# An MLP's late part in two tiles of 768 tokens instead of three of 512, and six attention blocks instead of eight with transposed exponentials

## Chip, cores and metric

The kernel runs on one core of a Trainium2 chip. The metric is the device time of one execution in microseconds (us), taken as the median of several runs. TensorE multiplies matrices, VectorE (DVE) and ScalarE (ACT) work elementwise and empty PSUM, GpSimd (POOL) helps with SBUF-only work, and all transfers are issued by SyncE (SP).

## What is computed

Sparse causal attention over q, k, v of shape (4, 8, 576, 64), then two MLPs over 2304 tokens of width 512 with a hidden width of 2048, the first with a squared relu, the second with a SiLU:

```python
scores = scale * np.matmul(q, k.transpose(0, 1, 3, 2))
mask_plain = (rel >= 0) & (rel < 32)                       # heads 0 to 3
mask_dil = (rel >= 0) & (rel < 128) & (rel % 4 == 0)       # heads 4 to 7
attn = softmax(where(mask, scores, -1e9)); x = attn @ v
...
h = x @ w_in;  r = np.maximum(h, 0.0);  x = (r * r) @ w_out
h = x @ w2_in; g = h * (1.0 / (1.0 + np.exp(-h))); out = g @ w2_out
```

The weights arrive as float64 words, and the kernel turns them into float32 itself.

## The kernel before

**Numbers.** Every large product is made of three matmuls on high and low halves (hi x hi, hi x lo, lo x hi; `fp32r` tiles). A value is split by a copy (ScalarE, mostly) into its high half and a subtraction (VectorE or GpSimd) for the low half.

**Attention.** 32 blocks (`attention(h, pair)`): h is half a batch entry (288 queries), pair two heads. Pairs 0 and 1 have three units of 96 queries with 96 to 128 keys, pairs 2 and 3 four units of 72 queries with 72 or 104 keys. An ordinary block computes scores on TensorE (L533), masks them and takes the row maximum on VectorE (L558), exponentiates each unit on ScalarE with the maximum as bias and the sum accumulated (L566), normalises (L586, L590, L592), transposes on TensorE (L602), copies back to SBUF and multiplies with v (L625). The first `EARLY` blocks go by `late_exp` (L680): scores are transposed first, the exponential of all units together is one instruction per group on ScalarE reading PSUM (L729), v has a column of ones so that the value product (L738) brings the sums along, and the result is normalised (L751, L754) and turned (L630). The maximum is subtracted beforehand on VectorE or GpSimd (`less`, L691 to L695) in the first `AHEAD` blocks, and by two more matmuls per unit (L717) in the other early ones. `EARLY` is 8 and `AHEAD` is 4, so blocks 0 to 3 subtract beforehand, blocks 4 to 7 by matmul, the others are ordinary.

**First MLP.** `TILES[0]` has three tiles of 256 tokens, which `mlp` (L771) runs interleaved chunk by chunk with attention and the conversion of the weights (`weights`, L255), and then three tiles of 512 tokens run by `mlp2` (L908). `mlp2` does its first product in seven Strassen products of 42 matmuls with 256 columns per pair of chunks (L936, eight pairs), assembles them on VectorE (`a1` to `a4`, L952), squares (L972), splits, and does the second product plainly with 192 matmuls of 512 columns (L990 to L992). Its inputs are prepared by `load_x` (L856).

**Second MLP.** Three tiles of 768 tokens run by `strassen` (L1054): both products have seven Strassen products, with matmuls of 384 columns (L1094 for the first, L1182 for the second). Sums of weight blocks for the first products are made by `sums` (L362), those for the second by `sums2` (L403), both written to DRAM and streamed in again (`stream`, L438, `stream2`, L468). `load_xs` (L1009) prepares the input and its differences.

**Order.** The order of all instructions is written out in the table `ORDER` (L1361): each word is an engine letter, the number of an operation in the order of its creation, and the places of its buffers. A word F means that many matmuls on a constant tile (L1248) whose results nobody reads. Places of SBUF buffers are given by the pools of L40 to L46.

## Time and profile before

| | |
|---|---|
| runs | 849.41 us median of 3 (848.76 to 850.98) |
| profiled execution | 851.04 us, of which the span from the first to the last instruction is 849.3 |
| busy: TensorE, VectorE, ScalarE, GpSimd | 840.2 (99%), 681.8 (80%), 501.2 (59%), 121.9 us (14%) |
| DMA | 222.49 MB by the queue that SP issues, 75.6% of 16 engines' span |
| chain that ended last | PE 94%, ACT 4%, DVE 1% |
| waiting matmuls (F words) | 53, all ahead of the first MLP step |

In the page's second part each digit is the busy share of one fortieth of the span in tenths. Matmuls are pipelined, so a single one's length is more than what it adds; the distance from one start to the next is what counts. The groups of rows name the line of the program, the engine, the operation and the tiles written and read.

### The profile page before, as it was taken

The numbers are of one execution on the slowest core, as the hardware profiler recorded it, in microseconds if no ns is written. First come the engines' busy times: TensorE is split into PE (matmuls) and PEld (weight loads), VectorE is DVE, ScalarE is ACT, GpSimd is POOL, SyncE is SP. The second block draws the span as 40 slices with busy tenths as digits, with TensorE's granted clock in tenths as the row PEclk, the third lists the DMA queues.
The fourth block names the chain that finished last, engine by engine and source line by source line (L and its number), as shares of the span: only waits on it lengthen the run. The fifth ranks groups of instructions, "written<-read, shape, count | busy, mean of one in ns | idle before, by whom it ended". The sixth has DMA issues, their size and how long they took to land.

```text
span 849.3 us, 17021 instructions
## 1 busy us (share of the span) xinstructions
PE 840.2 (99%) x6009; PEld 796.2 (94%) x6009; DVE 681.8 (80%) x1754; ACT 501.2 (59%) x1324; POOL 121.9 (14%) x142
## 2 busy tenths in 40 slices
PE   8999999999999999999999999999999999999998
PEld 7879999999989889889998999999999999999998
DVE  5999999888888698768899998898735788437865
ACT  4999988888566255324543466575445555345652
POOL 2211000101210202131201002202200111201120
PEclk9999999999999999999999999999999999999999
DMA  9486558779888888998999999889774675871751
GB/s 343 164 281 221 152 188 319 257 275 333 317 293 305 315 286 286 335 318 278 332 348 313 324 315 357 298 282 319 248 266 149 240 262 168 269 265 41 243 159 65
DMA packets 83604, 223.56 MB, mean 263 GB/s; under 512 B 8768, under 2 KB 18240, under 8 KB 83520
## 3 DMA queue, kind: packets, MB, share of 16 engines
q1 hardware_dynamic: 83520, 222.49, 75.6%
q8 instruction: 47, 0.77, 0.3%
q14 instruction: 37, 0.30, 0.1%
HBM read 172.13 MB, written 50.33 MB: 262 GB/s over the span
## 4 chain that ended last, share of the span: by engine, by line
PE 94%; ACT 4%; DVE 1%; DMA 0%; issue 0%; POOL 0%; SPq 0%; POOLq 0%; ACTq 0%
PE y L1094 17%; PE sa L1182 15%; PE s L936 14%; PE y L1182 6%; PE y L990 5%; PE y L991 5%; PE y L992 5%; PE sa L1094 4%; PE s L788 3%; PE s L789 2%; PE s L790 2%; PE ax L533 2%; PE y L836 2%; PE ax L625 2%; PE y L837 2%; PE y L838 2%
## 5 line engine op out<-in xcount | busy, mean ns | idle before, releaser
L245 ACT CAST hl<-gq 128x384 fp32r<-128x384 f32 x168 | 79.5, 513 | 62.7 <-PE sa L1182 27.0
L1094 PE MATMUL y<-xs,ws 128*128 128x384 f32 x552 | 107.5, 334 | 0.0
L1094 PEld LDWEIGHTS y<-xs,ws 128*128 128x128 f32 x552 | 96.7, 188 | 0.1
L252 DVE TENSOR_TENSOR hl<-gq,hl 128x384 fp32r<-128x384 f32 x144 | 78.7, 581 | 17.6 <-ACT hl L245 14.5
L1070 ACT COPY gq<-y 128x384 f32<-128x384 f32 x92 | 42.6, 479 | 69.1 <-PE y L1094 61.7
L1182 PE MATMUL sa<-hl,wp 128*128 128x384 f32 x432 | 79.1, 334 | 0.0
L936 PE MATMUL s<-x,ws 128*128 128x256 f32 x576 | 76.2, 284 | 0.0
L990 PE MATMUL y<-g,w 128*128 128x512 f32 x192 | 76.2, 397 | 0.0
L952 DVE TENSOR_TENSOR h<-s,h 128x512 f32<-128x512 f32 x96 | 59.5, 621 | 20.8 <-PE s L936 17.4
L1182 PEld LDWEIGHTS sa<-hl,wp 128*128 128x128 f32 x432 | 75.3, 188 | 0.0
L991 PE MATMUL y<-g,w 128*128 128x512 f32 x192 | 75.2, 391 | 0.0
L992 PE MATMUL y<-g,w 128*128 128x512 f32 x192 | 74.9, 390 | 0.0
L245 ACT CAST g<-r 128x256 fp32r<-128x256 f32 (+1 forms) x86 | 42.9, 504 | 52.0 <-DVE r L972 46.0
L936 PEld LDWEIGHTS s<-x,ws 128*128 128x128 f32 x576 | 72.2, 191 | 1.2
L566 ACT ACTIVATE ap<-ap,ast 96x128 f32<-96x128 f32 (+3 forms) x168 | 62.2, 372 | 8.3 <-DVE ast L575 4.2
L1065 DVE TENSOR_TENSOR gq<-y,gq 128x384 f32<-128x384 f32 x46 | 25.0, 554 | 52.0 <-PE y L1094 45.7
L788 PE MATMUL s<-x,w 128*128 128x256 f32 x192 | 56.3, 293 | 0.1
L1133 DVE TENSOR_TENSOR gq<-gq,sg 128x768 f32<-128x768 f32 x48 | 46.9, 992 | 10.3 <-ACT sg L1131 10.3
L790 PE MATMUL s<-x,w 128*128 128x256 f32 x192 | 54.3, 283 | 0.0
L789 PE MATMUL s<-x,w 128*128 128x256 f32 x192 | 54.2, 282 | 0.0
L1182 PE MATMUL y<-hl,sw 128*128 128x384 f32 x288 | 51.4, 334 | 0.0
L1182 PE MATMUL sa<-hl,sw 128*128 128x384 f32 x288 | 50.9, 334 | 0.0
(177 smaller groups left out, 2123.6 us busy)
## 6 DMA issues: line engine op xcount, KB each, us to landing
raw<-w SPq DMA_DIRECT2D x64, 512.0 KB, 6.1
ws<-w1x SPq DMA_DIRECT2D x48, 512.0 KB, 6.4
ws<-w2x SPq DMA_DIRECT2D x48, 512.0 KB, 5.4
sw<-w2y SPq DMA_DIRECT2D x48, 512.0 KB, 4.6
wa<-w1s SPq DMA_DIRECT2D x24, 512.0 KB, 6.9
wa<-w2s SPq DMA_DIRECT2D x24, 512.0 KB, 5.8
w1x<-st SPq DMA_DIRECT2D x16, 512.0 KB, 5.2
w2x<-st SPq DMA_DIRECT2D x16, 512.0 KB, 4.4
```

Of the source, the lines that this page charges most:

```text
L245: self.nc.scalar.copy(out=out, in_=in_)
L252: self.eng[eng].tensor_tensor(out=out, in0=a, in1=b, op=ALU.subtract)
L566: es.append(self.op({"ACT": c_act(nk) + 0.185}, lambda e, i=i, n=n, c=c, p=p, st=st: nc.scalar.activation(out=p.tile[:n, c], in_=p.tile[:n ...
L788: nc.tensor.matmul(o, wh.tile[:, s], xh, start=(kk == 0), stop=False)
L789: nc.tensor.matmul(o, wh.tile[:, s], xl, start=False, stop=False)
L790: nc.tensor.matmul(o, wl.tile[:, s], xh, start=False, stop=(kk == KC - 1))
L936: nc.tensor.matmul(bank.tile[:, o:o + 256], wp, xp, start=i == 0, stop=last, skip_group_check=True)
L990: nc.tensor.matmul(o, wh.tile[:, s], gh.tile, start=c == 0, stop=False)
L991: nc.tensor.matmul(o, wh.tile[:, s], gl.tile, start=False, stop=False)
L992: nc.tensor.matmul(o, wl.tile[:, s], gh.tile, start=False, stop=(c == NF - 1))
L1094: nc.tensor.matmul(o, w[part == 2].tile[:, kk * P:kk * P + P], x[b][part == 1].tile[:, kk * half:kk * half + half], start=new and not kk a ...
L1182: nc.tensor.matmul(o, u.tile[:, c * P:c * P + P], v.tile, start=new and not q and not part, stop=q == nf - 1 and part == 2, skip_group_che ...
```

## The change

The late part of the first MLP goes by `strassen` in two tiles of 768 tokens. Tile 3, which is in `WHOLE`, does its second product plainly in the new function `whole`, in two halves of 384 tokens; tile 4 does both products by Strassen. For that the second weight matrix of the first MLP is kept in SBUF in 256-column halves (`second`), its blocks are put together again (`again`), their sums are made and written to DRAM (`sums2(0, f)`) and streamed in for tile 4. `mlp2` and `load_x` go. `EARLY` is 6 and `AHEAD` 2: blocks 2 and 3 subtract the maximum by matmul, blocks 6 and 7 are ordinary. The squared relu may run on ScalarE in two steps (`relu2`). Pools and shared areas of SBUF are cut anew, and the order table is another one (4279 words instead of 4017; its F words ask for 86 matmuls, 41 ahead of the first MLP step and 45 behind it).

```diff
-EARLY = 8
-AHEAD = 4
+EARLY = 6
+AHEAD = 2
...
-TILES = ([(0, 256), (256, 256), (512, 256), (768, 512), (1280, 512), (1792, 512)], [(0, 768), (768, 768), (1536, 768)])
+TILES = ([(0, 256), (256, 256), (512, 256), (768, 768), (1536, 768)], [(0, 768), (768, 768), (1536, 768)])
...
-POOLS = {"u2": (8, 512), "u3": (2, 512), "u4": (28, 1024), "w1": (16, 1024), "blk": (BLK_BUFS, 1280)}
-SHARED_LO = 91
-SHARED_HI = 205
+POOLS = {"u2": (8, 512), "u4": (29, 1024), "w1": (16, 512), "w1o": (8, 1024), "blk": (BLK_BUFS, 1280)}
+SHARED_LO = 16
+SHARED_HI = 203
...
+    def again(self, j, c, key, gate):
+        b = self.spot(("cw", "ct")[j], PIECE)
+        old = self.kept[0, c, j, "c"]
...
+        elif j:
+            o = None
+            for i, (wh, wl, d) in enumerate(self.wt[0, 1, c]):
+                o = self.op({"Pool": c_pool2(256), "DVE": c_dve(256)}, lambda e, i=i, wh=wh, wl=wl: self.eng[e].tensor_tensor(
+                    out=b.tile[:, 256 * i:256 * i + 256], in0=wh.tile.bitcast(F32), in1=wl.tile.bitcast(F32), op=ALU.add), d + [o], key,
...
-    def sums2(self, f, key):
+    def sums2(self, m, f, key):
         nc = self.nc
-        (ca, wa), (cb, wb) = self.cv[2 * f], self.cv[2 * f + 1]
+        to = (self.w1y, self.w2y)[m]
+        (ca, wa), (cb, wb) = (self.cv[2 * f], self.cv[2 * f + 1]) if m else [self.again(1, c, key, key - T_LATER) for c in (2 * f, 2 * f + 1)]
...
-    def mlp2(self, m, t, k0, fetched):
...
         k0 += unit * nf
+        if m == 0 and t in WHOLE:
+            return self.whole(m, t, k0, done, g, chain, lag)
...
+    def whole(self, m, t, k0, done, g, chain, lag):
...
+        for s in range(2):
+            yb = [self.bank(f"y{e}") for e in range(KC)]
...
+            for c in range(NF):
+                q, i = c // 2, s + 2 * (c % 2)
...
+                h = self.op({"ACT": c_act(half)}, lambda e, src=src, hi=hi: self.copy(e, hi.tile, src()),
+                            [done["g", i % 2, q]], key - HL_LEAD, [hl], [g[q][i % 2]])
...
+                def s2(e, es, c=c, hi=hi, lo=lo, halves=halves, yb=yb):
+                    for ee in es:
+                        wh, wl, _ = halves[ee // 2]
+                        w = slice(ee % 2 * P, ee % 2 * P + P)
+                        for part, (u, v) in enumerate(((wh, hi), (wh, lo), (wl, hi))):
+                            nc.tensor.matmul(yb[ee].tile[:, :half], u.tile[:, w], v.tile, start=not c and not part,
+                                             stop=c == NF - 1 and part == 2, skip_group_check=True)
...
+        big = [(0, t) for t in range(FIRST, len(TILES[0]))] + [(1, t) for t in range(len(TILES[1]))]
+        self.load_xs(*big[0], start(*big[0]) - X1_LEAD)
+        for i, (m, t) in enumerate(big):
...
+            got = [self.stream(m, f, k + u * f - (S_AHEAD if m else W_AHEAD)) for f in range(NF // 2)]
+            if m or t not in WHOLE:
...
+                        if name in SUMS or (m and f >= KEPT):
+                            self.stream2(m, name, f, k + u * NF / 2 + u * (NF / 2) / 7 * (at + f / 8) - S2_AHEAD)
+            self.strassen(m, t, k, got)
...
+WHOLE = (3,)
```

## Rows read from the trace of the kernel before

**Rows 1.** The page's second part: busy tenths of two engines in 40 slices.
```profile
PE   8999999999999999999999999999999999999998
DVE  5999999888888698768899998898735788437865
```

**Rows 2.** Busy time by stage: length, busy us (count) of PE, PEld, DVE, ACT, POOL, clock, DMA.
```profile
26.00:75.00 49.00, 46.30 (x472) 42.40 (x471) 47.85 (x201) 46.73 (x152) 7.41 (x10) 1.00 0.69 231
75.00:141.00 66.00, 66.00 (x615) 62.87 (x613) 62.97 (x221) 60.31 (x203) 2.14 (x3) 1.00 0.59 204
...
217.50:482.40 264.90, 264.90 (x1911) 238.26 (x1910) 222.21 (x547) 124.75 (x350) 46.16 (x57) 1.00 0.89 311
482.40:607.50 125.10, 125.10 (x704) 122.62 (x703) 114.55 (x207) 72.66 (x145) 16.97 (x16) 1.00 0.89 308
```

**Rows 3.** TensorE in order of time, 512-token tiles: start us, length us, instructions.
```profile
370.11 0.40 PE L990 MATMUL y<-g,w 128*128 128x512 f32 x1
...
372.86 0.88 PE L936 MATMUL s<-x,wa 128*128 128x256 f32 x6
...
385.38 1.60 PE L936 MATMUL s<-x,wa 128*128 128x256 f32 x12
386.81 2.32 PE L936 MATMUL s<-x,ws 128*128 128x256 f32 x18
388.97 0.40 PE L990 MATMUL y<-g,w 128*128 128x512 f32 x1
```

**Rows 4.** The chain that ended last in order of time, 384-column matmuls: start, us, what.
```profile
571.15 8.32 PE sa L1182 x48
```

**Rows 5.** Groups by line and form, VectorE: count, busy us, mean ns, idle before.
```profile
L252 DVE TENSOR_TENSOR st<-st 128x512 fp32r<-128x512 f32 x45 | 31.0, 694 | 0.5 <-ACT st L245 0.4
...
L417 DVE TENSOR_TENSOR st<-cv 128x256 f32<-128x256 f32 x16 | 6.7, 430 | 0.2
```

**Rows 6.** Busy time of one stretch, columns as in rows 2.
```profile
476.00:498.00 22.00, 22.00 (x129) 19.96 (x128) 21.49 (x38) 10.84 (x20) 1.96 (x2) 1.00 0.88 306
```

**Rows 7.** TensorE in order of time, attention: columns as in rows 3.
```profile
17.20 0.41 PE L713 MATMUL ax<-ident,ap 72*72 72x72 f32 x4
...
55.31 0.27 PE L715 MATMUL ax<-ident,ap 72*104 72x72 f32 x1
...
56.34 1.40 PE L738 MATMUL ax<-blk,ap 104*72 104x65 f32 x16
57.54 0.36 PE L836 MATMUL y<-g,w 128*128 128x256 f32 x1
...
231.14 0.41 PE L602 MATMUL ax<-ident,ap 72*104 72x72 f32 x4
231.36 0.47 PE L990 MATMUL y<-g,w 128*128 128x512 f32 x1
...
233.23 0.72 PE L625 MATMUL ax<-ap,blk 104*64 104x72 f32 x16
```

**Rows 8.** ScalarE's exponentials: by form, then by line (least, median, most ns).
```profile
L566 ACT ACTIVATE ap<-ap,ast 72x104 f32<-72x104 f32 x48 | 17.8, 372 | 1.5 <-DVE ast L558 1.5
...
L729 ACT ACTIVATE ap<-ax x20: 238/406/436, 9.8 to 69.7; 128x192 f32<-128x192 f32 x4, 96x96 f32<-96x96 f32 x4, 72x288 f32<-72x288 f32 x4, 128x288 f32<-128x288 f32 x4
```

**Rows 9.** The very front in order of time, TensorE and VectorE: columns as in rows 3.
```profile
0.98 3.17 PE L1248 MATMUL fill<-warm 128*128 128x256 bf16 x14 [0.98 <-DVE warm L1240]
4.73 1.49 PE L533 MATMUL y<-w 64*96 64x96 f32 x12 [0.58 <-DMA w<-qkv]
...
6.36 0.29 DVE L558 CUSTOM_DVE_ANT_0 ap<-y,mask 96x128 f32<-96x128 f32 x1 [3.08 <-PE y L533]
10.61 0.29 DVE L558 CUSTOM_DVE_ANT_0 ap<-y,mask 96x128 f32<-96x128 f32 x1 [2.46 <-PE y L533]
...
25.82 0.36 PE L788 MATMUL s<-x,w 128*128 128x256 f32 x1
```

945 lines of the change are left out of this document (442 added, 503 removed).

## The prediction

> **What bounds the kernel now.** I read the two busy lines of the page first, then the busy time by stage, then single stretches. TensorE is at nine tenths or more in nearly every slice [rows 1]; the stages [rows 2] show why. From 217.5 to 482.4 us (the three 512-token tiles) it is busy for 264.90 of 264.90 us, with VectorE at 222.21, ScalarE at 124.75 and the DMA engines at a share of 0.89; in the second MLP up to 607.5 us it is again busy for all 125.10 us. There the number and the length of matmuls set the time. From 26 to 75 us it is otherwise: TensorE is busy for 46.30 of 49 us, VectorE for 47.85, ScalarE for 46.73. The two evictors bound that stretch, and TensorE work taken out of it alone gives nothing. From 75 to 141 us TensorE is the bound again (66.00 of 66 us), with VectorE close (62.97).
>
> **The late part: matmuls.** Removed are three 512-token tiles: 3 x 8 x 42 = 1008 matmuls of 256 columns for the first product (seven Strassen products) and 3 x 192 = 576 of 512 columns for the second (plain). Added are two 768-token tiles: 2 x 336 of 384 columns for the first product, 384 for the plain second product of tile 3 (`whole`), 336 for the Strassen second product of tile 4, in all 1392 of 384 columns. Start to start, 12 of 256 columns take 386.81 - 385.38 = 1.43 us and the next 18 take 2.16 us (119.2 and 120.0 ns each; I take 119.5), and 12 of 512 columns take 372.86 - 370.11 = 2.75 us (229.2 ns) [rows 3]; 48 of 384 columns take 8.32 us (173.3 ns) [rows 4]. So 1008 x 119.5 + 576 x 229.2 = 252.5 us become 1392 x 173.3 = 241.2 us: **-11.3 us**, on the engine that is never idle there.
> Where this comes from is worth seeing: 552,960 columns become 534,528. The slope between the 256 and 512 forms is 0.428 ns a column, so the columns alone are 7.9 us; the other 3.4 us are 192 matmuls fewer and the fixed part of each, about 10 ns by the same line.
> The rule that speaks against that second part: the Trainium skill, "TensorE: Matmul & The Clock Gate", section "Wait — 56ns, not 53.3ns?", gives N/2.4 GHz plus 2.5 ns, by which 109.2, 215.8 and 162.5 ns would stand for 119.5, 229.2 and 173.3, and the saving would be 8.2 us. The rows of this kernel are 10 to 13 ns longer in each form.
>
> **The late part: what hides beside it.** VectorE's elementwise work per tile is nearly the same (three times 30,720 columns of eviction against 33,800 for tile 3 and 55,300 for tile 4). New are the sums of the second weight matrix for tile 4 (`again`, `sums2(0, f)`): per f eight VectorE or GpSimd operations of 256 columns, two copies and two differences of 512, x8. At 6.7/16 = 0.42 us and 31.0/45 = 0.69 us busy [rows 5] that is 64 x 0.42 + 16 x 0.69 = 38 us if all ran on VectorE; the order table gives 63 of the 96 non-DMA steps of these sums to VectorE (about 25 us) and 20 to GpSimd. They stand between the first third of tile 3 and the start of tile 4, where by the order table VectorE has 0.7 to 0.95 us of work for each us of TensorE. Cover is there: VectorE was busy for 21.49 of 22 us from 476 to 498 us [rows 6] while TensorE lost nothing.
> DMA: 8 MB of sums stored and 8 MB loaded again are added, 14 MB of streamed first-product weights go (two tiles stream them, not three). The share of 0.89 [rows 2] stays about the same; I price it at 0, with 0 to +5 us as its bounds.
> Thinnest is the cover from tile 4's second product to the end of the second MLP's first first-product. Laid out by the order table with the start-to-start times above, VectorE has there 121 us of work beside 120 us of TensorE's, with no slack for 120 us. In the old table the same ratio holds from about 80 to 140 us, where TensorE was busy throughout [rows 2] and lost less than 1 us; but stretches of 1.08 (26 to 75 us) did cost. I take **+1 us**, bounds 0 and +10.
>
> **Attention, TensorE.** Blocks 6 and 7 (four units of 104 keys) turn from transposed-score to ordinary softmax. Removed per block: two transposes with the maximum subtracted by matmuls, 56.34 - 55.31 = 1.03 us each, and the value product, 57.54 - 56.34 = 1.20 us, with a turn (three or four transposes, I take 0.25 us as for those of 0.41 us length at 17.20); added: two plain transposes (231.36 - 231.14 = 0.22 us each) and the ordinary value product (0.72 us at most) [rows 7]. That is 3.5 against 1.1 us, -2.4 us a block, -4.8 us. Blocks 2 and 3 lose their subtraction on VectorE (`less`) and get the matmul form: four transposes of 1.03 us for four of at most 0.41, taken as 0.25 [rows 7], +3.1 us. Together **-1.7 us**. Both lie before 75 us, so by themselves they count only as far as the evictors allow.
>
> **Attention, evictors.** Ordinary blocks exponentiate unit by unit: 16 more instructions at 17.8/48 = 0.37 us [rows 8], 5.9 us, for four of 0.41 us [rows 8]; with the copies of the transposed scores and the changed normalising the order table gives ScalarE 5.9 us more for the two blocks, VectorE +0.7; without `less` VectorE has 1.4 less for blocks 2 and 3. The whole front is then laid out from both order tables: at the point where TensorE has 38 us of own work behind it, the new VectorE queue holds 5.7 us less than the old, at 86 us 3.6 more (ScalarE 5.6 more), at 123 us 4.0 more. The old VectorE ran 8.8 us behind its queue at the first MLP step (25.82 us, 17.0 us of work queued ahead) and stood still 2.3% of 26 to 75 us [rows 2, 9]. The same lag and idle share on the new queue put the 86-us point 1 us later than the old, 123 us at even. Since both evictors are now full together, I take **+2 us** for the start of tile 3, bounds -2 and +6. The table's own waiting matmuls point the same way: 86 instead of 53, of which 45 now stand after the first MLP step and none did before; at no more than the 0.12 us of a 256-column matmul each, some 5 us, TensorE is expected to wait there.
> The very front: 28 warm-up matmuls stand ahead of the first scores, not 14. At 3.17/14 = 0.226 us each [rows 9] they hold the scores until 0.98 + 6.3 = 7.3 us, not 4.73. But VectorE, which starts at 6.36 us now, then waits 2.46 us for the second scores behind 15 more such matmuls [rows 9], and in the new order those follow at once; by 10.6 us it has about the same work done. 0 us, bounds -1 and +1.
>
> **The sum.** -11.3 - 1.7 + 1 + 2 = -10.0 us. The profiled execution (851.04 us, span 849.3, so 1.7 us around it) becomes 841.0; the median of the runs, 849.41, stands 1.6 us below the profiled one, and becomes **839.4 us**.
>
> **The rivals.**
> A, the front costs nothing: the 5.7 us by which VectorE's queue is shorter early absorb the rest, and tile 3 starts 2 us earlier, not later: about 835.5. For it: the lower early queue; against it: the 45 waiting matmuls. 0.13.
> B, the front costs more: ScalarE and VectorE, both full, wait for each other, and tile 3 starts 6 us or more late: 844 to 846. The row for 26 to 75 us speaks for it, since 2.7 us went there already. 0.14.
> C, slower: from tile 4's second product on VectorE becomes the bound for 120 us, and the split of the next product's input (`hl`) reaches TensorE late. TensorE stood still for 2.7 of 49 us, 5.5%, where the evictors bound it before [rows 2]; the same share of 120 us is 6.6 us, 846.0 with the front as forecast. It decides for slower from some 11% on (13 us, 852.4), and 11 to 15% is 852 to 857. For it: no other stretch asks VectorE for all its time so long; against it: 476 to 498 us at 98% without a loss [rows 6]. 0.08 for slower, 0.05 for a loss that ends inside the bound of no change.
> D, DMA becomes the bound in the same stretch, where the order table asks for some 340 GB/s against 311 in the old stage [rows 2]: +5 us, 844. 0.04.
> E, the change doesn't save what it counts: the fixed part of a matmul goes along with the columns, so that only 18,432 x 0.428 = 7.9 us are saved: 842.8. The section of the Trainium skill named above would have it so. The straight line through the 256 and 512 forms gives 174.4 ns at 384, measured are 173.3 [rows 3, 4], so 0.03.
>
> **How the numbers follow.** My forecast, 836.5 to 843, has 0.53. A measurement of this kernel can tell about 0.3% from no change, that is 846.9 to 852.0 us. Faster than that: forecast 0.53, A 0.13, B 0.14 less 0.02 at its end, D 0.04, E 0.03: 0.85. Within: 0.02 + 0.05 = 0.07. Slower: 0.08. The range that leaves 0.2 out has to take in A's near side, all of B and D, and the near side of C: 834.5 to 848.
>
> **What would show each step.** The late part from the first `strassen` matmul of tile 3 to that of the second MLP should be some 11 us shorter than 264.9 us less any shift of attention, its 384-column matmuls 173 ns apart, and TensorE without idle. Tile 3's first matmul should come at 218 to 222 us, where the old one came at 217.5; before it TensorE should wait for ScalarE and VectorE between 40 and 80 us. If VectorE is above 97% busy in tile 4's second product and TensorE waits for `hl` there, C holds. If TensorE idles behind `sw` or `ws` loads, D does. I am wrong most likely in the front, where three engines are full at once and the sum is a difference of queues.

## The result: 0.7% slower, with the work saved as forecast

The changed kernel takes **854.32 us** (median of 18 runs, 851.26 to 862.83), the kernel before 849.11 us (18 runs beside them): a ratio of 1.0069 [1.0051, 1.0087]. Forecast were 839.4 us, with a range of 834.5 to 848.0. The forecast is wrong in sign.

Five of the 18 runs had a mean TensorE clock of 0.986 to 0.988 and took 859.3 to 862.8 us; the other 13 (clock 0.998 to 1.000) have a median of 853.33 us. So about 1 us of the 5.2 between the medians is those runs (the trace of `one_exp` below shows where such a run loses it), and 4.2 us is there at full clock. The profiled execution of after is one of the 13, at 852.6 us and a span of 850.8; that of before took 851.04 us and spans 849.3. The profiled pair therefore shows +1.5 us only. What the traces explain below is that pair; the other 2.7 us are the spread of single executions, which no trace shows.

The page of after, first its busy times, then the slices that answer to [rows 1], then the shares of its chain:

```profile
PE 834.3 (98%) x5842; PEld 807.4 (95%) x5842; DVE 686.9 (81%) x1825; ACT 583.4 (69%) x1494; POOL 104.6 (12%) x126
...
PE   8999999999999999999999999999999999999998
DVE  5999999988877899963799999999935787646874
PEclk9999999999999999999999999999999999999999
...
PE 79%; DVE 9%; ACT 5%; DMA 4%; issue 1%; SPq 0%; POOL 0%; ACTq 0%; DVEq 0%; POOLq 0%
```

By TensorE's digits nothing has changed: nine tenths everywhere. The loss is in pieces too small for them. The busy time by stage, cut at the same events as [rows 2] (columns as there):

```profile
26.00:75.00 49.00, 45.60 (x466) 40.17 (x465) 47.67 (x221) 48.26 (x176) 11.49 (x14) 1.00 0.74 241
75.00:141.00 66.00, 64.62 (x626) 60.50 (x626) 64.42 (x230) 62.12 (x212) 7.62 (x10) 1.00 0.68 221
...
224.70:486.20 261.50, 260.46 (x1680) 253.27 (x1679) 212.93 (x535) 186.60 (x450) 38.15 (x48) 1.00 0.89 311
486.20:612.00 125.80, 123.55 (x704) 121.38 (x703) 120.49 (x225) 87.19 (x170) 9.90 (x11) 1.00 0.90 315
```

The late tiles begin at 224.7 us, not 217.5 [rows 2], and TensorE's columns fall short of the lengths by 1.38, 1.04 and 2.25 us where before each stretch from 75 us on was full.

**An account of waits.** Busy time is a poor measure here: a matmul that waits inside a run of matmuls, a matmul at a lower clock and a matmul that only keeps the engine busy all count as busy. So I added up work instead. Each matmul is given its full-clock start-to-start time (0.1195 us for 256 columns, 0.1733 for 384, 0.2292 for 512, all from [rows 3, 4]; for the small attention forms the middle gap of their kind), the waiting matmuls are given none, and from a point in time the sum of all matmuls begun by then is taken off. What is left is the time in which TensorE did no work. The absolute value holds start-up and rounding; the differences carry the argument. (With the mean gap of the small forms in place of the middle one they move by up to 0.8 us: +7.9 at 224, +14.5 at the end.)

| not work, us, up to | 26 | 50 | 75 | 224 | 300 | 450 | 530 | end |
|---|---|---|---|---|---|---|---|---|
| before | 15.4 | 20.4 | 26.6 | 39.1 | 43.6 | 46.6 | 46.7 | 46.7 |
| after | 14.5 | 18.7 | 30.5 | 47.8 | 54.5 | 56.2 | 61.0 | 61.5 |
| after less before | -0.9 | -1.7 | +3.9 | +8.7 | +10.9 | +9.6 | +14.3 | +14.8 |

The work itself went from 799.0 to 785.6 us: -13.4, where the prediction's terms say -13.0. Waiting went up by 14.8. There are two places: 50 to 224 us (+10.4, of which 5.6 by 75 us) and 450 to 530 us (+4.7).

**What the first place looks like.** TensorE in order of time (start, length, instructions; in brackets idle time before, and what ended it), then SP's queue with the loads of blocks, and from the view of that tile their time to landing:

```profile
54.29 0.72 PE L658 MATMUL ax<-ap,blk 96*64 96x96 f32 x12
...
60.02 0.74 PE L566 MATMUL ax<-blk 64*72 64x72 f32 x16 [0.22 <-ACT ap L245]
60.69 0.72 PE L658 MATMUL ax<-ap,blk 104*64 104x72 f32 x16
61.34 1.70 PE L1195 MATMUL fill<-warm 128*128 128x256 bf16 x14
64.53 0.94 PE L1195 MATMUL fill<-warm 128*128 128x256 bf16 x7
65.60 0.63 PE L566 MATMUL ax<-blk 64*72 64x104 f32 x9
```
```profile
55.04 0.33 SPq L519 DMA_DIRECT2D blk<-qkv  x1
61.45 0.33 SPq L519 DMA_DIRECT2D blk<-qkv  x1
```
```profile
DMA to landing us min/median/max: 3.6/4.1/5.1
```

A chain closes here: the value product of a block at 60.69 frees its buffer, the load of the next block is issued at 61.45, lands some 4 us later, and the scores of that block start at 65.60. In between TensorE runs 21 waiting matmuls. Forty-five of them stand between 50 and 75 us, some 4.8 us in all at 0.107 us each, where before has none. What SP itself waits for from 40 to 90 us (us in total, times, longest) shows the link from value product (L658) to load:

```profile
SPq L519 <- PE ax L658: 23.8, 6, 5.7
```

Before has the same two buffers and the same link; there SP's waits for value products come to 15.3 us in that stretch, here to 25.6 with those of the early blocks. The chain is not new; SP stands longer in it. That this is what costs TensorE its time is a reading, which the experiments test.

**What the second place looks like.** The waits of TensorE by the group they wait for (us in total, times, longest) name only 2.3 of the 4.7 us; these two are the largest:

```profile
PE y L976 <- DMA wc<-w2s: 1.0, 1, 1.0
PE y L976 <- ACT gq L952: 0.7, 1, 0.7
```

The DMA queue of SP in order of time tells where the first comes from, with the matmul that waited:

```profile
517.36 1.59 SPq L1095 DMA_DIRECT2D y<-yq  x1
522.39 0.38 SPq L465 DMA_DIRECT2D w2y<-st  x1
522.81 0.56 SPq L1095 DMA_DIRECT2D y<-yq  x1
523.42 0.94 SPq L483 DMA_DIRECT2D wc<-w2s  x1
```
```profile
529.36 0.93 PE L976 MATMUL y<-xs,wc 128*128 128x384 f32 x4 [0.99 <-DMA wc<-w2s]
```

SP is through with one store at 518.95 and stands at the next, a store of weight sums (`st`) that VectorE hasn't finished, until 522.39. The load of `wc` is queued behind it and is issued at 523.42, and TensorE waits for it at 529.36. VectorE's last step for that store, in order of time, and then the stores of the sums that the change adds (count, least, median and most ns, first and last start):

```profile
521.67 0.69 DVE L252 TENSOR_TENSOR st<-st 128x512 fp32r<-128x512 f32 x1
```
```profile
L465 SPq DMA_DIRECT2D w1y<-st x16: 370/371/498, 274.7 to 393.1; - x16
```

The store that held the queue goes to `w2y`, the sums for the second MLP, of which before issues 16 as well (427.1 to 570.6 us there, 411.9 to 577.0 here). The 16 that the change adds go to `w1y` and are all out by 393.1 us. The load itself is under way for some 6 us, on full DMA engines; but they are as full in before, where TensorE loses nothing (busy time of ten us, before and then after):

```profile
520.00:530.00 10.00, 10.00 (x60) 10.00 (x59) 9.01 (x17) 5.82 (x12) 2.27 (x2) 1.00 0.98 340
```
```profile
520.00:530.00 10.00, 9.01 (x52) 8.66 (x52) 9.02 (x19) 8.18 (x15) 1.15 (x2) 1.00 1.02 353
```

### The profile page after: what moved, and what is told of

Its sections match the earlier page's. It is cut to its first block, busy times and chain, and to the rows that moved or that the text cites. A ratio compares the mean times of both kernels' runs of the same rounds, so it can differ in the third digit from the quotient of the medians.

```text
span 850.8 us, 16952 instructions
## 1 busy us (share of the span) xinstructions
PE 834.3 (98%) x5842; PEld 807.4 (95%) x5842; DVE 686.9 (81%) x1825; ACT 583.4 (69%) x1494; POOL 104.6 (12%) x126
## 4 chain that ended last, share of the span: by engine, by line
PE 79%; DVE 9%; ACT 5%; DMA 4%; issue 1%; SPq 0%; POOL 0%; ACTq 0%; DVEq 0%; POOLq 0%
PE y L976 26%; PE sa L1068 17%; PE y L1134 8%; PE y L1068 8%; PE sa L976 4%; PE s L821 2%; PE ax L566 2%; PE s L823 2%; PE s L822 2%; PE ax L658 2%; DMA blk<-qkv 1%; PE y L870 1%; PE ax L635 1%; PE y L872 1%; PE y L871 1%
## 5 line engine op out<-in xcount | busy, mean ns | idle before, releaser
L976 PE MATMUL y<-xs,ws 128*128 128x384 f32 x960 | 187.1, 336 | 1.3 <-ACT gq L952 0.7
L245 ACT CAST hl<-gq 128x384 fp32r<-128x384 f32 x256 | 121.1, 512 | 83.5 <-PE sa L1068 33.2
L976 PEld LDWEIGHTS y<-xs,ws 128*128 128x128 f32 x960 | 167.4, 188 | 3.0 <-ACT gq L952 1.3
L252 DVE TENSOR_TENSOR hl<-gq,hl 128x384 fp32r<-128x384 f32 x244 | 128.3, 555 | 22.6 <-ACT hl L245 22.0
L1068 PEld LDWEIGHTS sa<-hl,sw 128*128 128x128 f32 x384 | 66.5, 188 | 1.1 <-DVE hl L252 1.1
L1068 PEld LDWEIGHTS y<-hl,sw 128*128 128x128 f32 x384 | 66.7, 188 | 0.1
L252 DVE TENSOR_TENSOR gq<-gq 128x384 f32<-128x384 f32 x118 | 63.1, 558 | 0.1
L976 PE MATMUL y<-xs,wc 128*128 128x384 f32 x240 | 48.7, 337 | 1.0 <-DMA wc<-w2s 1.0
L976 PE MATMUL sa<-xs,wa 128*128 128x384 f32 x240 | 48.3, 335 | 0.3 <-DVE yq L947 0.3
L976 PE MATMUL y<-xs,wa 128*128 128x384 f32 x240 | 48.3, 335 | 0.0
```

The source lines that it names most:

```text
L245: self.nc.scalar.copy(out=out, in_=in_)
L252: self.eng[eng].tensor_tensor(out=out, in0=a, in1=b, op=ALU.subtract)
L976: nc.tensor.matmul(o, w[part == 2].tile[:, kk * P:kk * P + P], x[b][part == 1].tile[:, kk * half:kk * half + half], start=new and not kk a ...
L1068: nc.tensor.matmul(o, u.tile[:, c * P:c * P + P], v.tile, start=new and not q and not part, stop=q == nf - 1 and part == 2, skip_group_che ...
```

## Experiments

All medians stand beside runs of the kernel before on the same chip, which lay at 848.9 to 849.1 us. Where the edit is one to the order table, the diff names the steps that are moved in it. The kernels from `light_67` on start from `front_fill`, unless said otherwise, since it keeps the clock of the first 30 us up.

### Which half of the change: late part or attention

`late_alone` is after with eight blocks of the old kind, `att_alone` is before with six. Both have an order that I placed by hand.

```diff
 late_alone, against after
-EARLY = 6
-AHEAD = 2
+EARLY = 8
+AHEAD = 4
 att_alone, against before
-EARLY = 8
-AHEAD = 4
+EARLY = 6
+AHEAD = 2
```

> The changed kernel with the attention part undone: eight blocks with exponentials of transposed scores and four with the row minimum subtracted on VectorE, as before; tiles, weights and products of the late part as changed. By my instruction durations it has 11.2 us less TensorE work than the kernel before, the same ScalarE work before tile 3 (174.0 against 173.2 us) and 5.8 us more VectorE work there (197.9 against 192.1). Theory 1 (ScalarE's 5.9 us for blocks 6 and 7 delay the front, where ScalarE and VectorE are both about 97% busy): tile 3 starts 4 to 6 us sooner than in the changed kernel (about 218 to 220 us) and the time is 847 to 849. Theory 2 (VectorE's 5.8 us, or the tile of 768 tokens itself which wants a sixth half of attention before it starts, delays the front): tile 3 starts as late as in the changed kernel, the time is 851.5 to 855. The forecast as it stood for the late part alone: 842 to 843.

> The kernel before with the attention part of the change alone: blocks 6 and 7 in the ordinary form, blocks 2 and 3 with the row minimum taken off by TensorE; tiles and late part as before. By my instruction durations TensorE's work is 1.3 us less, VectorE's 0.9 us less, ScalarE's 5.8 us more. Theory 1 (ScalarE bounds the front): 3 to 5 us slower than the kernel before, 852 to 854, all of it lost before 112 us. Theory 2 (ScalarE has slack, the late part is what costs): 847.5 to 849.5.

871.25 us (866.6 to 876.1) and 863.11 us (862.1 to 866.3), ratios 1.0258 [1.0229, 1.0286] and 1.0169 [1.0152, 1.0187]. Both halves are slower than the whole, so for the total they tell one thing only: the hand-placed order (and a mean clock of 0.982 to 0.994 in all their runs) costs more than either edit, and the halves can't be added. What they do tell is place. By the account of waits, `late_alone` adds 6.9 us between 450 us and the end, `att_alone` 0.0 (60.4 at 450 and 60.4 at the end); its whole +13.7 comes before 450 us. So the second place belongs to the late part's two tiles and not to attention. For the first place they are inconclusive.

### Are the 45 waiting matmuls the loss, or its sign

```diff
 no_fill, order table, against after
-F1 F2 F1 F14 F7 F6 F12 F2   (eight entries between 50 and 75 us)
```

> The changed kernel without the eight groups of waiting matmuls (45 in all, at 0.107 us: 4.8 us) in its order table between the fifth and the tenth unit of the first tile. If they stand in TensorE's way: 2 to 4 us faster than the changed kernel, 850 to 852. If they fill time in which TensorE would wait anyway: the same within 1 us. If they hold TensorE's granted clock up: more runs with a granted clock of 0.99 or less and a time of 855 to 863.

857.17 us (854.6 to 863.9), 1.0107 [1.0079, 1.0135]. They are no loss of their own; without them the time goes up by about 3 us. The busy time of three stretches with the granted clock (the last number but two) shows what goes with their absence:

```profile
50.00:60.00 10.00, 8.32 (x74) 7.42 (x72) 9.60 (x46) 9.97 (x41) 1.92 (x2) 0.83 0.76 216
60.00:70.00 10.00, 7.17 (x89) 6.11 (x90) 9.95 (x51) 9.87 (x46) 2.55 (x3) 0.88 0.59 206
70.00:80.00 10.00, 9.20 (x73) 8.27 (x73) 8.92 (x41) 8.33 (x35) 2.37 (x3) 0.60 0.93 276
```

The clock falls to 0.83, 0.88 and 0.60 where after has 1.00 throughout 26 to 75 us, and the matmuls that come then run longer. With nothing to fill them, TensorE's waits can be read by name (50 to 100 us; the two largest):

```profile
PE ax L658 <- ACT ap L245: 2.1, 3, 1.0
PE y L871 <- DVE g L252: 1.0, 1, 1.0
```

In all 3.9 us are for ScalarE and 1.9 for VectorE; none is named for a block's load.

### Is it ScalarE's load

```diff
 one_exp, against after (blocks 6 and 7)
-    nc.scalar.activation(...)      # four units, one instruction each
+    nc.scalar.activation(out=x, in_=x, func=AF.Exp, scale=-1.0)   # once over all units
```

> The changed kernel, but blocks 6 and 7 take one exponential over all four units of a head where they took four, without the row minimum and the row sums (this changes what is computed). ScalarE is relieved by 4 x (4 x 0.37 - 0.44) = 4.1 us in the front, nothing else is changed. Theory 1 (ScalarE bounds the front): tile 3 starts 3 to 4 us sooner, 850 to 851.5 against the changed kernel's 854.3. Theory 2 (VectorE or the wider tile): less than 1 us.

857.09 us (852.38 to 863.06). Three of six runs took 859.7 to 863.1 at a mean clock of 0.986 to 0.988; the other three, 852.38, 853.52 and 854.44, lie where after's 13 lie (853.33). So relief of ScalarE alone gives nothing measurable. The profiled execution is one of the three at the lower clock, and it shows where that happens:

```profile
0.00:10.00 10.00, 7.84 (x73) 5.92 (x73) 3.50 (x29) 1.49 (x2) 3.94 (x13) 1.00 0.82 277
10.00:20.00 10.00, 9.94 (x82) 9.33 (x80) 6.25 (x52) 5.72 (x19) 1.94 (x2) 0.55 0.73 257
20.00:30.00 10.00, 9.94 (x75) 9.04 (x75) 5.50 (x21) 6.28 (x20) 0.00 (x0) 0.50 0.72 234
30.00:40.00 10.00, 9.57 (x72) 8.73 (x73) 8.62 (x32) 8.15 (x19) 1.95 (x3) 0.76 0.57 230
```

In the first 10 us TensorE is busy for 7.84 us; then the clock stands at its lower level (0.50, 1.2 GHz) until some 35 us. From 10 to 30 us it runs 157 matmuls in this execution, and 212 in after's.

### Does the very front need more waiting matmuls

```diff
 front_fill, order table, against after
+F3@1   (ahead of the third unit's scores, att0.2.score)
+F7@1   (ahead of the first transposes, att0.0.0.transp)
```

> The changed kernel with ten more waiting matmuls in its first 11 us: three ahead of the scores of block 2 and seven ahead of the first transpose, where TensorE stood idle 0.28, 0.26 and 0.64 us in the changed kernel's trace. Of that kernel's 18 runs five had a granted clock of 0.986 to 0.988 and took 859.3 to 862.8 us; the thirteen others, at 0.998 to 1.0, took 851.3 to 855.9, in the middle 852.6. If these idle times let the clock fall: no run of this kernel under 0.99, all within 851 to 856. If something else does: one or two of six runs at 0.986 and 859 to 863, as before. Either way the undisturbed runs stay at 852 to 854, since nothing else is changed.

854.47 us (852.29 to 857.39), 1.0063 [1.0047, 1.008]. The expectation gives 852.6 as the middle of after's 13 runs; it is 853.33. The lower clock in the front is gone: of the 53 runs of this kernel and of the eight later ones that keep the 45 waiting matmuls, the lowest mean clock is 0.996. The median is no better than after's 854.32, and 1.1 us above that of its 13 runs, inside the spread of either kernel. The account is after's up to 450 us (14.0 at 26 us, 56.1 at 450), and 8.5 us from there to the end where after has 5.3, with the same steps: so much single executions differ in the late stretch.

### Is it the load of the two new ordinary blocks, or of any block

`light_67` leaves the softmax out of blocks 6 and 7, `light_5` out of blocks 22 and 23, which come later (half 5, pairs 2 and 3): raw scores are copied in one instruction, so that VectorE and ScalarE are relieved and TensorE's work stays.

```diff
+LIGHT = ((1, 2), (1, 3))      # light_67;   ((5, 2), (5, 3)) in light_5
-    nc.vector.tensor_tensor_reduce(...)
+    self.raw_scores(...) if (h, pair) in LIGHT else nc.vector.tensor_tensor_reduce(...)
-    nc.scalar.activation(...)
+    (h, pair) in LIGHT or nc.scalar.activation(...)
```

> As front_fill, but attention blocks 6 and 7 lose their softmax (raw scores are copied and transposed; this leaves out the minimum, the exponentials, the sums and the scaling): about 2.9 us of VectorE and 8 us of ScalarE less before 75 us; TensorE's work is the same. Theory 1 (the front is bound by what VectorE and ScalarE must do before tile 3): 2.5 to 4 us faster than front_fill. Theory 2 (TensorE waits in the front for the length of chains, not for full engines): 1 us or less, as the kernel with one exponential for four showed for ScalarE alone.

> As front_fill, but the last two blocks of half 5, which the tile of 768 tokens needs before it starts and the tile of 512 did not, lose their softmax in the same way: about 2.9 us of VectorE and 8 us of ScalarE less between about 170 and 215 us. Theory 1 (load of VectorE and ScalarE before tile 3): 2.5 to 4 us faster than front_fill, tile 3 that much sooner. Theory 2 (chains and the order): 1 us or less.

852.13 us (851.12 to 853.58), 1.0036, and 853.95 us (852.1 to 857.6), 1.006. Blocks 6 and 7 are worth 2.3 us of `front_fill`'s 854.47; blocks 22 and 23, whose load is of the same kind, 0.5, which is inside the spread. In `light_67` the account stands at 29.1 at 75 us and 46.1 at 224, 1.0 and 1.3 under `front_fill`. So the load of the new softmaxes is a part, and the smaller one: before stands at 26.6 and 39.1.

### Is it VectorE's load

`light_v` replaces the subtraction that makes the low parts of the first MLP's weights by a copy, over the whole front; `light_67n` is `light_67` without the 45 waiting matmuls; `light_v67n` is both. If the waiting matmuls only bridge waits, they can go once the waits are gone.

```diff
 light_v (the first MLP's weights only)
-    self.sub(e, lv(), cs(), hv().bitcast(F32))
+    self.copy(e, lv(), cs())
```

> As front_fill, but the low parts of the first MLP's weights are plain copies and not subtractions (values change, this leaves the subtractions out): 34 operations of VectorE before tile 3 at about half their time, 3.1 us less by the start of tile 1 and 7.6 us less by tile 3; nothing else changes. If VectorE is what bounds the front: 3 to 7 us faster than front_fill (854.5; undisturbed runs 852.3). If not: less than 1 us.

> As light_67 (blocks 6 and 7 without their softmax, which leaves that out) but also without the 45 later waiting matmuls, 4.8 us of TensorE between 51 and 74 us. Theory 1 (the waits that these matmuls fill come from blocks 6 and 7's work on VectorE and ScalarE): with that work gone nothing is left to fill, TensorE goes on with real work, 3 to 5 us faster than light_67's 852.1, that is 847 to 849, and the granted clock stays at 1.0. Theory 2 (the waits come from what has to be done in the front anyway): no faster than light_67, 852 to 858, with the granted clock fallen between 50 and 80 us as in the kernel without the waiting matmuls.

> light_v and light_67n together: about 6 us of VectorE and 8 us of ScalarE less by the start of tile 1, 10.5 us of VectorE less by tile 3, and no waiting matmuls after 30 us (the softmax of blocks 6 and 7 and the subtractions are left out). If load on the two engines is what makes TensorE wait in the front, most of the 9.6 us that the changed kernel lost between 26 and 224 us comes back: 843 to 847. If not: 850 or more.

854.69 (853.8 to 856.1), 855.93 (853.8 to 856.7) and 856.91 us (853.3 to 859.0). The theories of a single full evictor fall: VectorE's relief gives nothing, and with both relieved the 45 matmuls still can't be left out. In `light_v67n` VectorE is at 8.41 us of ten and ScalarE at 6.53, and TensorE still waits and loses its clock (busy time of two stretches, then one row of TensorE in order of time):

```profile
60.00:70.00 10.00, 8.04 (x70) 6.83 (x67) 8.41 (x35) 6.53 (x29) 1.70 (x3) 0.57 0.51 176
70.00:80.00 10.00, 9.38 (x73) 8.71 (x72) 6.60 (x37) 6.54 (x26) 1.78 (x3) 0.58 0.89 274
```
```profile
64.99 1.73 PE L567 MATMUL ax<-blk 64*72 64x104 f32 x16 [0.70 <-DMA blk<-qkv]
```

What ended this wait is the load of `blk`, the buffer chain of the first place. It is one of three in these ten us; the other two, 0.77 and 0.48 us, are for VectorE and for ScalarE.

### Is it the block buffers

`third_blk_n` lets eight of the block loads go round four places in SBUF, not two, and issues them 25 to 46 entries of the order table earlier, so that they don't wait for a value product; the 45 waiting matmuls are left out. `third_67n` adds the light softmax of blocks 6 and 7, `third_light_n` the light weights of `light_v` as well.

```diff
 third_blk_n, order table: the loads of blk 1.2, 2.2, 1.3, 2.3, 3.0, 3.1, 3.2, 3.3
-D462@201   (behind the release of the buffer)
+D462@180   (28 entries earlier, at a free place; the other seven alike)
-F1 F2 F1 F14 F7 F6 F12 F2
```

> As front_fill, but the loads of eight attention blocks (1.2 to 3.3) are issued 30 to 55 places earlier into SBUF that stood free, so that three or four blocks are held and not two, and the 45 later waiting matmuls are gone. In the changed kernel each of these loads was issued 0.8 us after the end of the block but one before (46.3 to 47.1, 54.3 to 55.0, 60.7 to 61.5, 67.7 to 68.5, 75.5 to 76.3 us) and landed 4 us later, and the scores began as it landed. Theory B (two block buffers set the pace of the front between 43 and 82 us, and the waiting matmuls fill that): 2 to 5 us faster than front_fill and the granted clock at 1.0. Theory C (the chain of a block through VectorE and ScalarE sets it, in the order as it stands): no faster than the kernel without the waiting matmuls (857.2), with the clock fallen as there.

> third_blk_n (early block loads, no waiting matmuls after 30 us; 857.4) with the softmax of blocks 6 and 7 left out, but with the subtractions of the first MLP's low parts in place. third_light_n, which leaves both out, took 851.3. If it is the work of blocks 6 and 7 on VectorE and ScalarE, together with the two buffers, that makes TensorE wait between 50 and 80 us: 851 to 853. If the subtractions of all the weights (3.1 us of VectorE by the start of tile 1) matter as much: 854 to 856. If neither alone does anything: 857.

> third_blk_n with the softmax of blocks 6 and 7 and the subtractions of the first MLP's low parts left out as in light_v67n (856.9 us), where four waits for block loads of 0.6 to 1.6 us stood between 58 and 98 us. Theory B (with VectorE and ScalarE relieved, the two buffers are what is left): these waits go, 4 us or more faster than light_v67n, 848 to 853. Theory C: within 2 us of it.

| | buffers | blocks 6, 7 light | weights light | us | ratio to before |
|---|---|---|---|---|---|
| `no_fill` | | | | 857.17 | 1.0107 [1.0079, 1.0135] |
| `light_67n` | | yes | | 855.93 | 1.0073 [1.006, 1.0086] |
| `light_v67n` | | yes | yes | 856.91 | 1.0088 [1.0071, 1.0105] |
| `third_blk_n` | yes | | | 857.43 | 1.0097 [1.0083, 1.0111] |
| `third_67n` | yes | yes | | 852.19 | 1.0038 [1.0023, 1.0053] |
| `third_light_n` | yes | yes | yes | 851.26 | 1.0026 [1.0017, 1.0035] |

None of these six has the 45 waiting matmuls (the first lacks the ten of `front_fill` too). Against `no_fill` the buffers alone give 0, the light softmax alone 1.2 us, both together 5.0 us. That would fit two limits of nearly equal length: the next block's scores wait for its data and for the evictors' earlier work, and taking one away leaves the other. But with the 45 waiting matmuls kept, the light softmax alone takes 852.13 us (`light_67`), as much as `third_67n` with 852.19: the early loads bring no more than the waiting matmuls do, and against `front_fill` both kernels gain 2.3 us. Part of the 5.0 us is the clock. The same stretch in `third_67n`, then in `third_blk_n`:

```profile
60.00:70.00 10.00, 6.46 (x74) 5.20 (x68) 10.00 (x39) 8.25 (x33) 2.55 (x3) 1.00 0.88 351
70.00:80.00 10.00, 9.31 (x107) 8.28 (x108) 9.80 (x41) 8.56 (x31) 2.17 (x3) 1.00 0.74 237
```
```profile
60.00:70.00 10.00, 8.05 (x83) 6.79 (x80) 10.00 (x52) 9.35 (x43) 2.55 (x3) 0.83 0.80 322
70.00:80.00 10.00, 7.31 (x72) 6.64 (x72) 9.24 (x42) 8.61 (x37) 2.18 (x3) 0.83 0.73 239
```

From 60 to 80 us one runs 181 matmuls at 1.00, the other 155 at 0.83. In `third_67n` TensorE is idle for 3.5 us of 60 to 70, VectorE for none. Its waits named between 50 and 100 us are for ScalarE (3.0 us) and VectorE (2.4 us), none for a block's load. In `third_light_n`, with the weights light too, the account stands at 44.1 at 224 us, 3.7 of the 8.7 us back. The other 5 us are still there, though VectorE has only 195.8 us of work up to 224 us, against 201.6 before (ScalarE 186.8 against 185.4). **They are not explained**: the order of the steps is the same as in after, and I didn't plan it anew for these kernels.

### Is the late loss VectorE's load, or full DMA rings

`light_late` replaces the subtractions of the sums for the second MLP's weights, and of its first tile's input, by copies. `light_dma` cuts the second `ws` load of the first eight streamed weight steps of the second MLP to a quarter, 256 of 1024 columns.

```diff
 light_late
-    self.sub(...)
+    self.copy(e, v(1), v(0).bitcast(F32)) if m else self.sub(...)
 light_dma
+    if few and i > 1:
+        view, src = (lambda t: t[:, :256]), src[:, :256]
```

> As front_fill, but the subtractions that make the low parts of the sums of the second MLP's weights, and the low parts and differences of the second MLP's first tile of x, are plain copies (values change, this leaves the subtractions out): about 7 us of VectorE less in about 400 to 612 us, where VectorE was busy 110.7 of 116 us; all else is as it was. Theory V (VectorE bounds the stretch from 489 to 555 us, and its late stores hold the loads): 3 to 4 us faster than front_fill. Theory D (the DMA queue by itself is late, VectorE only full): less than 1 us.

> As front_fill, but for the first tile of the second MLP the second of the two loads of weight sums of each pair brings 256 columns, not 1024, and four operands are taken from them (values change): 8 x 384 KB = 3.1 MB less traffic, about 8.6 us of the DMA rings at 360 GB/s, all about 440 to 560 us. In light_late, with VectorE relieved, TensorE still waited 1.3, 1.0 and 0.3 us for loads of w2s and w2x, and the rings were 0.97 to 1.03 busy. Theory D (the rings are full from 490 to 555 us): the waits for wc and ws between 500 and 550 us go, 1.5 to 3 us faster than front_fill. Theory V (VectorE's late stores hold the queue): the waits stay, less than 1 us.

852.40 us (850.63 to 855.15), 1.0041 [1.0026, 1.0057], and 851.63 us (850.26 to 855.9, nine runs), 1.0037 [1.0023, 1.0051]: 2.1 and 2.8 us under `front_fill` by the medians, with intervals that still overlap its own. By the account, `light_late` adds 5.0 us from 450 us to the end and `light_dma` 6.1, where the two kernels without these edits add 5.3 and 8.5. Neither comes near 0.1, the value of before. In `light_late` VectorE is busy for 188.4 us from 400 to 612 us, against 193.9 before and 197.6 in after: its amount of work lies below that of before, and the late loss stays. By its median `light_dma` lies in what theory D expected, by its trace it doesn't. With VectorE relieved the waits move to loads (`ws` 0.26, `wc` 1.26, `ws` 1.03 us). With less to load TensorE waits longer in one piece, though the queue's own wait is the same kind as in after (busy time of ten us, two rows of SP's queue, TensorE's wait for the tile: us, times):

```profile
520.00:530.00 10.00, 7.41 (x42) 6.85 (x41) 7.52 (x15) 6.70 (x14) 0.72 (x1) 1.00 0.97 345
```
```profile
521.34 0.38 SPq L465 DMA_DIRECT2D w2y<-st  x1
522.33 0.78 SPq L488 DMA_DIRECT2D wc<-w2s  x1
```
```profile
  DMA wc<-w2s: 2.6, 1
```

The load of `wc` is issued at 522.33, behind a store of sums, and TensorE waits 2.6 us for it. Loading less did not remove the wait for a load that was issued late. Its DMA engines are still full in those ten us (0.97), so their part in the time that the load takes is not tested.

### Is it the order on the DMA queue

`sp_order` puts eight loads for the second MLP's first products ahead of four groups of stores; `third_sp` is `sp_order` with the early block loads; `sp_place` is `sp_order` with the stores' sources moved to places that the next products' copies don't use.

```diff
 sp_order, order table
+D3008@40 D2999@0              (wc, ws: ahead of the stores T1.4)
+D3003@4 D3009@124 D3012@80    (ahead of T1.5)
+D3013@104 D3016@100 D3011@2   (ahead of S1.7, W1.15)
 sp_place, besides
-V2014@112 V2012@84 A1870@68 V2038@96 V2040@100
+V2014@172 V2012@176 A1870@180 V2038@184 V2040@172
```

> As front_fill, with eight loads of weights for the first tile of the second MLP issued ahead of the stores of sums that stood before them in the DMA queue; nothing else moves. In the changed kernel the queue stood from 518.95 to 522.39 us at a store that waited for VectorE's sums, the load of wc behind it was issued at 523.42, and TensorE waited 0.99 us for it at 529.4 (2.6 us in front_fill and light_dma, whose trace showed the rings only 0.74 to 0.97 busy there). Theory Q (the order of the queue, not VectorE's load and not the rings): the waits for wc and ws between 500 and 550 us go, 1.5 to 3 us faster than front_fill (median 854.5, undisturbed 852.3). Theory D (full rings): the same as front_fill within 1 us.

> The early block loads of third_blk_n with the 45 waiting matmuls kept, and the queue order of sp_order; output as the changed kernel's. With the waiting matmuls in place theory B expects little in the front (less than 1.5 us), theory Q 1.5 to 3 us behind 500 us: 850 to 852.5. If both are nothing: 852.5 to 855.

> sp_order with five buffers of sums and weights (three of about 500 to 512 us, two of about 516 to 525 us) put at SBUF places that stood free, so that ScalarE's copies of partial products no longer take the places that the held stores have to free; queue order and all else as in sp_order, output as the changed kernel's. In sp_order ScalarE's copy waited 3.9 us for a store of sums at 514.5 us and TensorE 4.5 us for that copy, and the time was 859.4 against front_fill's 854.5. Theory P (the late waits come from the queue's one order together with shared places: loads first hold the stores that free ScalarE's buffers, stores first hold TensorE's weights): both waits go, 850.5 to 853. Theory R (rings or VectorE are the bound after all): 856 or more.

859.37 us (856.1 to 859.9), 857.37 us (856.4 to 860.8) and 857.16 us (855.7 to 857.9); ratios 1.0106, 1.0103 and 1.009, each with an interval of under 0.002 to either side. The remedy is worse than the wait. (`third_sp`, the one kernel with the early block loads and the 45 waiting matmuls kept, lies 2.0 us under `sp_order` by the medians, and their runs overlap.) In `sp_order` TensorE's wait for `wc` is gone, and ScalarE, then TensorE, in order of time show what came in its place:

```profile
513.92 0.62 ACT L245 CAST st<-cv 128x512 fp32r<-128x512 f32 x1 [1.47 <-POOL cv L318]
...
518.46 0.48 ACT L952 COPY gq<-y 128x384 f32<-128x384 f32 x1 [3.91 <-DMA w2y<-st]
...
518.99 1.33 PE L976 MATMUL y<-xs,ws 128*128 128x384 f32 x3 [4.48 <-ACT gq L952]
```

The copy `gq` writes to a place that the store of sums still has to read. The store is now later, the copy waits 3.91 us for it, and TensorE 4.48 us for the copy. With the places changed, in `sp_place`, TensorE's wait for that copy is 0.28 us, and a later copy meets another store, of the first MLP's results, in the same way (ScalarE in order of time, then the waits of TensorE):

```profile
532.50 0.48 ACT L952 COPY gq<-y 128x384 f32<-128x384 f32 x1 [4.05 <-DMA y<-yq]
```
```profile
PE y L976 <- ACT gq L952: 4.2, 2, 3.9
```

`sp_place` gains 2.2 us on `sp_order` and is still 2.7 above `front_fill`. What is shown: neither of these two orders helps, since a load moved ahead makes a copy wait for the store that it passed. What isn't: that no order would.

## Why the prediction was wrong

**The late part's matmuls: right.** Priced at -11.3 us from 119.5, 229.2 and 173.3 ns. In after's chain in order of time (start, us, what) an unbroken run of the new form is

```profile
307.66 31.20 PE y L1134 x180
```

that is 173.3 ns each. With the counts of the trace the late part's matmuls are 241.2 us against 252.5 before. The stage of the late tiles is only 3.4 us shorter (261.5 against 264.9 us [rows 2]), because the cut moved through it: 60 matmuls of 512 columns (13.8 us) lie behind it before, 42 of 384 (7.3 us) after; with them it is 268.8 against 278.7. Rival E (the fixed part is not saved) falls, by its own row. One reading of the prediction is off: 192 matmuls fewer at about 10 ns are 1.9 us, not 3.4; the other 1.5 us are the 1.1 ns by which the row of 384 columns lies under its straight line, 1392 times. The 162.5 ns that the Trainium skill, "TensorE: Matmul & The Clock Gate", section "Wait — 56ns, not 53.3ns?", leads to for 384 columns stays 10.8 ns under the 173.3 measured; the saving by that rule, 8.2 us, is near E's 7.9 and not the same.

**Attention's TensorE work: right.** Forecast -1.7. Over the whole kernel the work fell by 13.4 us, of which the late part's matmuls are 11.3; so attention's is about 2.1 us less. (Tile 3's first matmul came 7.2 us later with 8.7 us more waiting by then, so the work ahead of it is 1.5 us less; but that is another sum, with two more blocks of attention ahead of it and 24 matmuls of 256 columns behind it that stood ahead before.)

**The front: the step that failed.** It was "+2 us for the start of tile 3, bounds -2 and +6", and 218 to 222 us for its first matmul; measured are +8.7 and 224.74 us. I laid out VectorE's and ScalarE's queues, found 4.0 and 5.6 us more work, and took the old lag and idle share for the new queue. That is what failed: up to 224 us VectorE and ScalarE are busy for 200.5 and 190.8 us, against 201.6 and 185.4 before, and TensorE waits 8.7 us more. The sum has no term for a chain that goes round through engines: value product, release of the block's buffer, load (4.1 us to landing), scores, softmax on VectorE and ScalarE, value product. Ahead of tile 3's first matmul TensorE's rows of before hold 96 transposes of ordinary blocks (L602), those of after 128 (L635): 32 more, two for each of the 16 units of four blocks. Two are blocks 6 and 7, two more belong to half 5, since a tile that ends at token 1536 needs all of that half (tokens 1440 to 1727) and one that ended at 1280 needed none of it. I had counted their queue time, and not that each holds one of the two buffers until its value product. The runs show that no single one of the chain's links carries the loss: relief of ScalarE (`one_exp`) and of VectorE (`light_v`) give 0 each, light blocks 6 and 7 give 2.3 us; without the waiting matmuls the buffers alone give 0 (`third_blk_n`) and buffers with light blocks 5.0 us. They don't show that the chain is the cause: what ends TensorE's waits in `no_fill` is ScalarE and VectorE, not a load. That engines are full by turns, which a price by queue sums can't see, fits all of this and stays a reading. The row that should have warned was named: "45 now stand after the first MLP step and none did before", some 5 us. I read the order table's own waiting matmuls as agreeing with +2 when they stood for some 5. They come to 4.8 us, and that is about the rise from 50 to 75 us (5.6).

**Rival B** ("the front costs more: ScalarE and VectorE, both full, wait for each other", 6 us or more, 844 to 846) came true in place and size, and had 0.14: tile 3 starts 7.2 us late, and the waits named in `no_fill` are for those two engines. That they wait for each other is not shown. Its total was still too low, since the next term was missing.

**Tile 4's second product on: inside its bounds, five times its value.** Taken as +1, bounds 0 to +10; measured +5.2 from 450 us to the end. The working behind it was right, 121 us of VectorE's work beside 120 us of TensorE's: from 430.8 to 554.9 us VectorE is busy for 120.45 of 124.10 us, 97%. Rival C said that VectorE would be the bound and `hl` late; the wait for `hl` was 0.3 us. It did not come true as put, and `light_late` shows it, since with VectorE relieved 5.0 us stay (5.3 and 8.5 without). Rival D said full DMA engines: the share rose from 0.89 to 0.90 only, and `light_dma` left 6.1 us. What I had left out is a term between the two: a store on SP's queue that waits for VectorE holds back the loads behind it. I had priced stores as VectorE time and as bytes, and not as entries in a queue that is served in order. The rows show it for one load, 1.0 of the 5.2 us. It doesn't come from the stores that the change adds, which are out by 393.1 us; the one that held the load is among those that before has too. Why it costs here and not there, and where the rest goes, stays open. ScalarE, busy for 147.9 us from 400 to 612 us against 113.0 before, was relieved there in no run.

**The sum.** -13.4 of work (forecast -13.0), +8.7 in the front (+2), +0.9 from 224 to 450 us (0), +5.2 behind (+1): +1.4, where the spans say +1.5. Forecast and measured differ by 11.5 us in the profiled pair, of which 6.7 is the front and 4.2 the late stretch.

**What stays open**: 5 of the 8.7 us in the front, which no relief that I tried gave back; what the step order itself has in it, since the order table moved other steps too (the first store to `w1s` is issued at 50.8 us, before at 30.8) and no run has a newly planned one; the cause of the late loss; the 2.4 us of late waiting that no view names; and why the median lies 2.7 us further from before than the profiled pair does. No version ran faster than the kernel before; the nearest, `third_light_n`, leaves work out and is still 0.26% slower.

## To carry to other kernels

Where TensorE is full, price a change of tile shape by start-to-start times from rows; here it came out within half a microsecond. Where three engines are nearly full, a difference of queue sums is no price: here the queues grew by up to 5.6 us and TensorE lost 8.7, which relief of one engine didn't give back. Follow one buffer round its loop (release, issue, landing, use) as well, and widen the bounds. Take an order table's own waiting matmuls as a statement of how long it expects to wait, and don't forecast less. For a store that waits for an engine, name the loads queued behind it; moving them ahead lengthens the time for which the store's source has to stay where it is, and here that cost more than it gave.

## What the runs showed of the hardware

**The clock can fall after waits that are each under a microsecond.** The first matmuls of after, in order of time:

```profile
8.61 0.34 PE L566 MATMUL y<-bl 64*72 64x72 f32 x2 [0.28 <-DVE ast L591]
9.21 0.73 PE L566 MATMUL y<-bl 64*72 64x72 f32 x14 [0.26 <-DVE ast L591]
10.82 0.38 PE L746 MATMUL ax<-ident,ap 96*128 96x96 f32 x2 [0.64 <-POOL ap L727]
```

In this execution the clock stayed up. The trace of `one_exp` has the same waits, 0.28, 0.26 and 0.64 us, ahead of a granted clock of 0.50 to 0.55 from 11 to 35 us. Three of the six runs of `one_exp` and 5 of 18 of after have the mean clock that goes with it (0.986 to 0.988) and are some 8 us longer, the others of the same kernels not; for after's five no trace shows the place. With ten waiting matmuls there, no run of 53 had a mean clock under 0.996. The Trainium skill, "TensorE: Matmul & The Clock Gate", section "A second HAM failure mode: psum-queue depth-cycling", tells of short idle spells between groups of matmuls that make the clock swing between its two levels; the trace agrees that short spells go with it, and shows one fall and one rise, in some runs only.

**Waiting matmuls can be worth their place.** Without the 45 in the front the kernel is some 3 us slower (857.17 against 854.32 us), and the rows show a clock of 0.60 to 0.88 between 50 and 80 us beside it. With light blocks 6 and 7 it is 3.8 us (855.93 against 852.13), and the runs of the two kernels don't overlap.
